# A fused linear-attention and gated-MLP kernel on one core: in blocks 3 to 6, four of the seven products of a Strassen-type step are summed in one PSUM half bank

## The chip, the cores and the metric

The kernel runs on one NeuronCore of one Trainium2 chip. The metric is the device time of one execution in microseconds, as the median of several runs. Of the kernel before there are three runs: 1049.51, 1049.64 and 1049.84 us, median 1049.64 us. One more execution was taken with the hardware profiler; it took 1050.2 us, of which 1048.4 us lie between its first and its last instruction (the span).

## The reference

Random-feature attention, then a gated MLP without an activation. All data are float32.

```
attention: q, k, v are (8 batches, 8 heads, 576 tokens, 64), omega is (128, 64)
  phi(x) = exp(h - max(h)) / sqrt(128),  h = x omega^T - |x|^2 / 2,  x = q or k, scaled by 64^-0.25
  kv = phi(k)^T v      z = sum over tokens of phi(k)
  out = phi(q) kv / (phi(q) z + 1e-6)
MLP: x is the attention's output as (4608 tokens, 512)
  y = ((x w_a) * (x w_b)) w_out,   w_a and w_b are 512 x 1536, w_out is 1536 x 512
```

## The kernel before

**Blocks.** The MLP runs over blocks of 512 tokens on TensorE (PE), one for each of the eight batches (b = 0 to 7), and a ninth (b = 8) that gathers the last 64 tokens of every batch. Every float32 operand is split into a high and a low part, and a product is made of three matmuls (high x high, high x low, low x high). Blocks 0 and 1 (`moe_block`, L1188) multiply plainly. Blocks 2 to 8 (`moe_block7`, L1263) form the two inner products x w_a and x w_b, in 2 x 2 sub-blocks of 256, by a Strassen-type scheme with seven products in place of eight. The sums of the weights that the scheme needs are made once (`weight_sums`, L1230), stored in DRAM and loaded again by every unit (tiles `t` and `bq`); the sums of the tokens are the tiles `Sa` and `Sb`.

**A unit** (`unit`, L1273) is one pair of 128-wide feature groups of one of the two weights: 12 units in a block. Each of its seven products (`product`, L1293) is six matmuls of 128 x 256 into one half (256 columns) of one of two PSUM banks, `p0` and `p1` (`halves`). The products of all units form one chain in their order (list `prev`), and each also waits until everything that reads its bank so far has read it (`pb.readers`, L1302). The order in a unit is: first into p0 half 0, copied by ScalarE (ACT) to the SBUF tile `c4` (L1313); second into p1 half 0 and third into p1 half 1; a VectorE (DVE) add of 512 columns over p1 (L1317); fourth into p0 half 1 and fifth into p0 half 0; a DVE add of 512 and one of 256 columns over p0 (L1326, L1328); sixth and seventh into p1, and a DVE add of 512 columns (L1333). So a unit has one ACT copy and four DVE adds, and the four results stand in `c4`.

**Items.** After both units of a pair, DVE multiplies the two `c4` (L1358), the result is split into `ghl` (L1361, `hilo` L1181), and eight items are put into a list `left`: an item is three matmuls of 128 x 512 that multiply `ghl` by `wo` into the output banks `o` (`Out.mm`, L1010). `flush` (L1220) takes items out of the list in order and gives them to the planner at certain places of a unit: L1320 (1, or 5 in the first unit of a block), L1329 (1) and L1335 (2; in blocks 7 and 8 it is 1), none in the last unit of a block. Blocks 7 and 8 use another output (`Out7`, L1049), whose items are products of six matmuls of 128 x 256, and one product `one` (L1126, in list `ones7`) that goes into `p1` in the midst of the next unit and needs the tile `wo`.

**Attention.** The attention for the next batches is done in bursts (`burst`, L685) that are put between units at places fixed in the table `PLACE`. A burst holds the numerator of an earlier pair (L878), kv (L804), and the projections of 8 chunks of 128 tokens (`four`, L528, twice, 16 matmuls each). Bursts 12 to 31 (`MERGED`) use `p0` and `p1` for the first `four` and stand in the chain of products; ACT (or DVE) copies the projections out of them. At the last head pair of a batch (hp1 == 0, L717) the burst also makes the projections of the next batch's last tokens, `last_chunks` (L675), a third call of `four` on banks of its own (`ppke` and `ppqe`, ring `at`), which the planner places where it finds room; the next burst waits for it (`carry["e"]`, L688).

**The order of the work** is made by a planner on the host (`Graph`, L63 to L296) when the kernel is built. Every operation has a cost in ns (`mm` L299 for matmuls, `dve` and `act` for the others), engines that may run it, a priority and its dependences. The planner simulates the engines with these costs, always starts what can start first and breaks ties by priority (PE) or by due time (DVE, ACT, POOL), plans four times and keeps the plan whose simulated end is earliest. The program issues each engine's instructions in that order; on the chip an engine's queue is in order. Between a projection burst and other work the planner prefers the next piece of the same burst, up to 700 ns (`GLUE`).

The lines that the text speaks of most:

```
def mm(n, cols):
    return n * max(112, 7 + 0.441 * cols)
...
flush(seq + 3, 5 if i == w == 0 else k)
...
if hp1 == 0:
    last_chunks(b1, pr + 15, xe, sqe, lead, mg)
```

## Time and profile before

| what | value |
|---|---|
| median of three runs | 1049.64 us (1049.51 to 1049.84) |
| the profiled execution | 1050.2 us |
| its span, first to last instruction | 1048.4 us |
| PE busy (matmuls) | 1034.0 us, 99% of the span |
| DVE busy | 899.6 us, 86% |
| ACT busy | 588.9 us, 56% |
| mean granted clock of PE | 0.994 |
| DMA | 314.16 MB, 300 GB/s |

The profiled execution stands 0.6 us above the median of the runs. A matmul's end is modelled in the profile: the difference between two starts tells how fast PE goes, the duration of one does not. Busy shares are means over stages, so the profile is read by block: blocks 2 to 8 begin at about 300, 411, 523, 634, 746, 849 and 947 us.

### The profile page before, as it was taken

How to read it: one execution, taken by the hardware profiler on the slowest of the kernel's cores; microseconds unless marked ns; L12 is line 12 of the kernel's file. 1: busy time of each engine (PE TensorE's matmuls, PEld its weight loads, DVE VectorE, ACT ScalarE, POOL GpSimd, SP SyncE). 2: the span in 40 equal slices, each digit the busy share in tenths (PEclk: the TensorE clock that was granted, in tenths of full speed). 3: DMA queues.
4: the chain of work that ended last, by engine and by line, in shares of the span. 5: the costliest groups of instructions: out<-in, count | busy, mean ns of one | idle time of the engine just before them, and what ended most of it. 6: DMA issues, size and time to landing. Idle time of an engine off the chain costs nothing.

```text
span 1048.4 us, 22053 instructions
## 1 busy us (share of the span) xinstructions
PE 1034.0 (99%) x7806; PEld 916.1 (87%) x7806; DVE 899.6 (86%) x2255; ACT 588.9 (56%) x1629; POOL 109.5 (10%) x177
## 2 busy tenths in 40 slices
PE   9999999999999999999999999999999998999998
PEld 8877777777788988999999998899989998999998
DVE  6999999899997889888998888888887666999876
ACT  8989798868565646765566556654552023233221
POOL 0112111202101111111111111101010000000000
PEclk9989999999999999999999999999999999999999
DMA  9857878898989999998899988998788787899981
GB/s 353 324 200 249 294 237 261 313 330 297 306 304 384 355 286 323 325 352 301 302 311 357 311 303 268 352 304 291 254 310 280 262 277 256 309 359 349 367 323 49
DMA packets 123647, 314.16 MB, mean 300 GB/s; under 512 B 17680, under 2 KB 40976, under 8 KB 123536
## 3 DMA queue, kind: packets, MB, share of 16 engines
q1 hardware_dynamic: 122656, 312.10, 85.7%
q8 instruction: 61, 1.00, 0.4%
q10 hardware_dynamic: 880, 0.66, 0.2%
q14 instruction: 50, 0.41, 0.1%
HBM read 255.52 MB, written 57.18 MB: 298 GB/s over the span
## 4 chain that ended last, share of the span: by engine, by line
PE 82%; DVE 12%; DMA 2%; issue 2%; ACT 2%; DVEq 0%; ACTq 0%
PE p L1298 39%; PE o L1016 18%; PE o_P L1086 5%; PE pa L1206 3%; PE pb L1206 3%; PE ppk L540 3%; PE pkv L804 2%; PE pm L878 2%; PE p L540 2%; DVE sm L565 1%; DMA td<-ts 1%; DVE raw L419 1%; DVE zero L824 1%; PE p L1086 1%; PE pn L950 1%
## 5 line engine op out<-in xcount | busy, mean ns | idle before, releaser
L1308 DVE TENSOR_TENSOR c<-p,c 128x512 f32<-128x512 f32 (+1 forms) x336 | 207.6, 618 | 69.6 <-PE p L1298 56.2
L1016 PE MATMUL o<-wo,ghl 128*128 128x512 f32 x1008 | 249.5, 393 | 0.0
L1016 PEld LDWEIGHTS o<-wo,ghl 128*128 128x128 f32 x1008 | 183.5, 188 | 37.7 <-issue 0.9
L1298 PE MATMUL p<-Sa,t 128*128 128x256 f32 x1008 | 132.6, 280 | 0.7 <-ACT c L365 0.7
L1298 PEld LDWEIGHTS p<-Sa,t 128*128 128x128 f32 x1008 | 124.5, 188 | 1.3 <-ACT c L365 1.1
L758 POOL TENSOR_TENSOR z<-hk 128x256 f32<-128x256 f32 x56 | 46.1, 824 | 632.7 <-ACT hk L578 496.9
L834 ACT ACTIVATE hq<-hq,dn 128x128 f32<-128x128 f32 x224 | 70.1, 390 | 45.1 <-DVE dn L830 44.9
L365 ACT COPY c<-p 128x256 f32<-128x256 f32 x84 | 31.1, 370 | 102.1 <-PE p L1298 98.9
L1206 PE MATMUL pa<-x,wa 128*128 128x512 f32 x288 | 76.2, 408 | 2.1 <-DVE x L373 2.1
L1206 PE MATMUL pb<-x,wb 128*128 128x512 f32 x288 | 74.9, 403 | 0.6 <-ACT wb L365 0.3
L1298 PE MATMUL p<-x,t 128*128 128x256 f32 x504 | 74.3, 283 | 0.9 <-ACT oc L365 0.7
L1298 PE MATMUL p<-Sb,bq 128*128 128x256 f32 x504 | 74.3, 283 | 0.0
L1298 PE MATMUL p<-Sb,t 128*128 128x256 f32 x504 | 73.5, 282 | 0.0
L578 ACT ACTIVATE hq<-hq,sm 128x128 f32<-128x128 f32 x192 | 64.4, 392 | 15.3 <-DVE sm L573 15.2
L824 DVE CUSTOM_DVE_ANT_0 zero<-hq,zb 128x128 bf16<-128x128 f32 x224 | 69.2, 309 | 1.0
L1298 PE MATMUL p<-x,wa 128*128 128x256 f32 x504 | 69.1, 283 | 0.2 <-DVE c L1308 0.2
L1298 PE MATMUL p<-x,wb 128*128 128x256 f32 x504 | 69.0, 282 | 0.0
L1298 PEld LDWEIGHTS p<-x,wa 128*128 128x128 f32 x504 | 65.3, 188 | 3.7 <-DVE c L1308 0.8
L1206 PEld LDWEIGHTS pa<-x,wa 128*128 128x128 f32 x288 | 54.4, 193 | 16.0 <-DVE x L373 2.4
L1298 PEld LDWEIGHTS p<-x,t 128*128 128x128 f32 x504 | 66.5, 190 | 2.0 <-ACT oc L365 0.9
L1298 PEld LDWEIGHTS p<-x,wb 128*128 128x128 f32 x504 | 65.2, 189 | 3.1 <-DVE c L1308 0.4
L1206 PEld LDWEIGHTS pb<-x,wb 128*128 128x128 f32 x288 | 53.2, 189 | 15.4 <-DVE a L1214 1.1
(202 smaller groups left out, 2025.5 us busy)
## 6 DMA issues: line engine op xcount, KB each, us to landing
t<-td SPq DMA_DIRECT2D x168, 512.0 KB
wo<-wod SPq DMA_DIRECT2D x96, 512.0 KB
bq<-bd SPq DMA_DIRECT2D x84, 256.0 KB
qdr<-qd SPq DMA_DIRECT2D x112, 160.0 KB
hq<-qdr SPq DMA_DIRECT2D x28, 640.0 KB
X<-in_kqt_dram SPq DMA_DIRECT2D x30, 512.0 KB
raw<-in_wab_dram SPq DMA_DIRECT2D x24, 512.0 KB
td<-ts SPq DMA_DIRECT2D x24, 512.0 KB
```

The lines of the kernel that those rows point to most:

```text
L365: nc.scalar.copy(o(), i())
L540: nc.tensor.matmul(flat4(pps[w])[:, c * M:c * M + M], x()[rows, c * P:c * P + P], om.ap[rows], start=True, stop=True)
L578: g.op({"ACT": 392}, lambda e, c=c, w=w, to=to, at=at: nc.scalar.activation(to.ap[:, at + c], src[w](c), AF.Exp, scale=SC, bias=sm.ap[:, 2 ...
L758: g.op({"POOL": pool2(n)}, lambda e: nc.gpsimd.tensor_tensor(o(), a(), c(), op=ALU.add), r=r, w=w, alloc=list(al), prio=pri, deps=zload[-1 ...
L804: nc.tensor.matmul(pkv.ap[D * j:D * j + D, 0:M], vb.ap[:, vc, 0:D], c(), start=(n == 0), stop=(n == 4))
L824: g.op({"DVE": 413}, lambda e, c=c, j=j, rr=rr, qc=qc: nc.vector.tensor_tensor_reduce(out=junk.ap[rr], in0=qc(), in1=zb.ap[rr, j], scale=1 ...
L834: g.op({"ACT": 392}, lambda e, c=c, src=src: nc.scalar.activation(hq.ap[:, c], src(), AF.Copy, scale=dn.ap[:, c:c + 1]), r=[sd, (dn, None) ...
L1016: nc.tensor.matmul(po.ap[:], ghl.ap[:, gi, t * P:(t + 1) * P], wo.ap[:, wi], start=(n == 0 and i == 0), stop=(n == NF - 1 and i == 2))
L1086: nc.tensor.matmul(pb.ap[:, t], A[0](ai)[:, t * P:(t + 1) * P], W[0](wi), start=begin and t == j == 0, stop=stop and t == 1 and j == 2)
L1206: nc.tensor.matmul(pb.ap[:], wt.ap[:, wi, c], xs[c].at(xi), start=(c == 0 and i == 0), stop=(c == NC4 - 1 and i == 2))
L1298: nc.tensor.matmul(pb.ap[:, half], wcol(wi, c), xc(xi, c), start=n == 0, stop=n == 5)
L1308: g.op({"DVE": dve(n)}, lambda e: nc.vector.tensor_tensor(c4.ap[:, o], pb.ap[:, half], y(), op=ALU.add), r=[*((pb, k) for k in range(half. ...
```

## The change

Three things are changed. The new settings `PSH`, `PSUMS`, `PLO`, `SUBX` and `SNAP` stand at 0 or empty, and what hangs on them is as before.

1. In blocks 3 to 6 (`CHAIN`) a unit's products go another way. First, sixth, seventh and eighth step below all go into p0 half 0 without clearing it, so that the bank holds a running sum; after each, ACT copies the half bank to one quarter of `c4` (four copies of 256 columns). The other three go into p1, and DVE adds them to `c4` (one add of 512 columns, one of 256). The first unit of such a block gives the planner 3 items at L1320 where it gave 5; the others give what they gave.
2. `last_chunks` gets the banks `p0` and `p1` in merged bursts and stands in the chain right behind the burst's second `four`. This holds for bursts 15, 19, 23 and 27.
3. The planner's cost of a matmul: 117.8 ns for 256 columns (119.9 before) and 228.3 ns for 512 (232.8 before), for all blocks.

```diff
 def mm(n, cols):
-    return n * max(112, 7 + 0.441 * cols)
+    return n * (117.8 if cols == 256 else max(112, 4 + 0.438 * cols))
...
-            def product(pb, half, wcol, wr, xc, xrd, pos):
+            def product(pb, half, wcol, wr, xc, xrd, pos, begin=True):
...
-                            nc.tensor.matmul(pb.ap[:, half], wcol(wi, c), xc(xi, c), start=n == 0, stop=n == 5)
+                            nc.tensor.matmul(pb.ap[:, half], wcol(wi, c), xc(xi, c), start=begin and n == 0, stop=n == 5, skip_group_check=not begin)
...
+            if b not in CFG["CHAIN"]:
...
+            def snap(q, al=()):
+                g.op({"ACT": act(HM), **{k: dve(HM) for k in CFG["SNAP"]}}, copier(lambda: c4.ap[:, q], lambda: p0.ap[:, 0]), r=[(p0, 0)], w=[(c4, q)],
+                     alloc=list(al), prio=-12)
+            def add(o, half, parts):
+                n = HM * (half.stop - half.start)
+                g.op({"DVE": dve(n)}, lambda e: nc.vector.tensor_tensor(c4.ap[:, o], p1.ap[:, half], c4.ap[:, o], op=ALU.add),
...
+            wait = 3 if i == w == 0 else 0
+            def first():
+                steps.append(product(p0, 0, lambda k, c: f0.ap[:, k, c], (f0, None), xcol(0, lo_half), xr(0), 0))
+                snap(0, [c4])
+            def second():
+                product(p1, 0, lambda k, c: f0.ap[:, k, 2 + c], (f0, None), xcol(2, lo_half), xr(2), 1)
+            def sixth():
+                product(p0, 0, tcol(tA, 0), (tA, None), scol(1), sr[0], 2, False)
+                snap(2)
+            def fifth():
+                product(p1, 1, tcol(tA, 1), (tA, None), scol(0), sr[0], 4)
+            def seventh():
+                product(p0, 0, tcol(tB, 0), (tB, None), scol(2), sr[1], 5, False)
+                snap(3)
+            first()
...
+                second()
+                sixth()
+                flush(seq + 3, wait or k)
+                fifth()
+                seventh()
+            add(slice(0, 4, 3), slice(0, 2), (0, 3))
             flush(seq + 6, k)
+            product(p0, 0, tcol(tB, 1), (tB, None), xcol(2, hi_half), xr(2), 7, False)
+            snap(1)
+            product(p1, 1, lambda k, c: bq.ap[:, k, P * c:P * c + P], (bq, None), scol(3), sr[1], 8, False)
+            add(slice(2, 3), slice(1, 2), (2,))
...
             if hp1 == 0:
-                last_chunks(b1, pr + 15, xe, sqe, lead, mg)
+                last_chunks(b1, pr + 15, xe, sqe, [*lead, *chain()], mg, banks() if merged else None)
+                glue(place if merged else None, carry["e"])
+                if merged:
+                    carry.pop("e")
```

## Rows read from the trace of the kernel before

**Rows 1.** The page's head: the span, and the busy time, share and instructions of each engine.

```profile
span 1048.4 us, 22053 instructions
PE 1034.0 (99%) x7806; PEld 916.1 (87%) x7806; DVE 899.6 (86%) x2255; ACT 588.9 (56%) x1629; POOL 109.5 (10%) x177
```

**Rows 2.** Busy time of each engine by stage (from:to, length, then busy us and number of instructions), the granted clock of PE (1.00 is 2.4 GHz, 0.50 is 1.2 GHz), the DMA share and GB/s. Blocks 2, 3, 4, 5, 6 and 7.

```profile
300.20:410.80 110.60, 109.66 (x893) 98.47 (x891) 94.13 (x246) 68.05 (x195) 13.95 (x24) 1.00 0.95 326
410.80:522.70 111.90, 111.90 (x906) 101.11 (x906) 96.47 (x265) 67.75 (x193) 13.77 (x24) 1.00 0.92 324
522.70:634.10 111.40, 111.40 (x906) 101.13 (x905) 96.82 (x262) 65.17 (x189) 14.33 (x24) 1.00 0.92 317
634.10:745.70 111.60, 111.60 (x906) 101.00 (x905) 95.47 (x258) 61.99 (x183) 15.13 (x24) 1.00 0.90 303
745.70:848.90 103.20, 103.20 (x769) 93.57 (x768) 74.30 (x169) 34.68 (x99) 4.39 (x6) 1.00 0.83 279
848.90:946.60 97.70, 94.44 (x739) 91.70 (x739) 82.84 (x171) 29.31 (x66) 0.00 (x0) 0.98 0.87 303
```

**Rows 3.** Whom PE waited for in the whole execution: us in total, times, longest. The largest rows that bear on the change.

```profile
PE p L1086 <- DMA wo<-wod: 2.1, 1, 2.1
PE pa L1206 <- DVE x L373: 2.1, 1, 2.1
...
PE p L1298 <- ACT c L365: 0.7, 1, 0.7
PE p L1298 <- ACT oc L365: 0.7, 1, 0.7
```

**Rows 4.** PE's matmuls in blocks 3 to 6 (410.8 to 848.9 us), grouped: busy us and mean ns of one, then PE's idle time just before them.

```profile
L1016 PE MATMUL o<-wo,ghl 128*128 128x512 f32 x577 | 143.2, 394 | 0.0
L1298 PE MATMUL p<-Sa,t 128*128 128x256 f32 x576 | 75.5, 280 | 0.0
```

**Rows 5.** DVE and ACT in blocks 3 to 6, in the same form: the DVE adds of a unit, its ACT copy, and three frequent neighbours on ACT.

```profile
L1308 DVE TENSOR_TENSOR c<-p,c 128x512 f32<-128x512 f32 x145 | 99.1, 683 | 33.9 <-PE p L1298 30.0 <-ACT hq L834 1.1 <-ACT hq L578 1.0
L1308 DVE TENSOR_TENSOR c<-p,c 128x256 f32<-128x256 f32 x48 | 19.8, 413 | 0.8
...
L365 ACT COPY c<-p 128x256 f32<-128x256 f32 x48 | 17.6, 368 | 48.5 <-PE p L1298 45.5 <-DVE c L1358 2.7
L834 ACT ACTIVATE hq<-hq,dn 128x128 f32<-128x128 f32 x120 | 37.6, 390 | 30.1 <-DVE dn L830 30.1
L365 ACT CAST ghl<-c 128x512 fp32r<-128x512 f32 x16 | 9.9, 620 | 14.7 <-PE o L1016 10.1 <-issue 3.0 <-DVE c L1358 1.4
```

**Rows 6.** One unit on PE in block 4, in order of time: start us, length us, what. The first row is two products, the second two, the next two one each; the fifth is four items, and the last begins the next unit.

```profile
563.59 1.58 PE L1298 MATMUL p<-x,wa 128*128 128x256 f32 x12
565.01 1.57 PE L1298 MATMUL p<-Sa,t 128*128 128x256 f32 x12
566.41 0.88 PE L1298 MATMUL p<-Sb,t 128*128 128x256 f32 x6
...
567.84 0.88 PE L1298 MATMUL p<-Sb,bq 128*128 128x256 f32 x6
568.56 2.88 PE L1016 MATMUL o<-wo,ghl 128*128 128x512 f32 x12
571.28 1.56 PE L1298 MATMUL p<-x,wb 128*128 128x256 f32 x12
```

**Rows 7.** From a product to its ACT copy, and from an ACT copy to the product that waited for it: timelines of PE and of ACT in block 2. The bracket is the engine's idle time before, and what ended it.

```profile
321.05 1.60 PE L1298 MATMUL p<-x,wa 128*128 128x256 f32 x12
...
321.96 0.37 ACT L365 COPY c<-p 128x256 f32<-128x256 f32 x1 [0.92 <-PE p L1298]
...
316.31 0.35 ACT L365 COPY c<-p 128x256 f32<-128x256 f32 x1
...
316.71 0.97 PE L1298 MATMUL p<-Sa,t 128*128 128x256 f32 x6 [0.69 <-ACT c L365]
```

**Rows 8.** The end of burst 19's pair, nine items, the last tokens' projections (`ppke`, `ppqe`) and three items, on PE; and ACT's copies of the burst's first `four` out of p0 and p1 (`hk<-p`, `hq<-p`).

```profile
559.20 0.27 PE L540 MATMUL ppq<-om,X 64*128 64x128 f32 x1
559.40 2.36 PE L1016 MATMUL o<-wo,ghl 128*128 128x512 f32 x9
561.69 0.37 PE L540 MATMUL ppke<-om,Xe 64*128 64x128 f32 x1
...
562.46 0.27 PE L540 MATMUL ppke<-om,Xe 64*128 64x128 f32 x1
...
562.57 0.27 PE L540 MATMUL ppke<-om,Xe 64*128 64x128 f32 x1
...
562.78 0.97 PE L1016 MATMUL o<-wo,ghl 128*128 128x512 f32 x3
...
558.65 0.59 ACT L365 COPY hk<-p 128x512 f32<-128x512 f32 x1 [0.74 <-issue]
559.13 0.59 ACT L365 COPY hq<-p 128x512 f32<-128x512 f32 x1
```

**Rows 9.** Stages as in rows 2, around the two longest waits of PE: right after the wait at 53.8 us, and right after the one that ends at 873.75 us.

```profile
54.00:58.00 4.00, 4.00 (x10) 3.12 (x11) 3.97 (x10) 3.74 (x11) 0.81 (x2) 0.50 0.46 161
...
873.75:876.00 2.25, 1.57 (x9) 1.37 (x10) 0.00 (x0) 0.58 (x1) 0.00 (x0) 0.80 0.90 331
876.00:878.10 2.10, 2.10 (x11) 2.10 (x11) 0.00 (x0) 0.00 (x0) 0.00 (x0) 0.50 0.34 124
```

More of the change, by code (lines that the diff above doesn't have):

```diff
@@ L528, in four @@
     def four(nm, b, pri, x, xdep, dst, c0, sm, sq, al, deps, mg, more, banks=None):
-        own = banks is None
+        own, less = banks is None, b in CFG["SUBX"]
         pps = [g.buf("at", [P, 4 * M], F32, f"pp{'kq'[w]}{nm}{c0}", more) for w in range(2)] if own else banks
@@ L574, in four @@
         g.op({"DVE": 300}, biases, r=[(sm, (c0, 0)), (sm, (c0, 1)), (psq if sq is None else sq, None)], w=[(sm, (c0, 0)), (sm, (c0, 1))], prio=pri + 2)
-        for w in range(2):
+        for w in range(2) if less else ():
+            to, at = dst[w]
+            whole = (lambda pp=pps[w]: wide4(pp)) if not (b >= B1 or not own) else (lambda to=to, at=at: to.ap[:, at + c0:at + c0 + 4])
+            mine = lambda to=to, at=at: to.ap[:, at + c0:at + c0 + 4]
+            done = [(to, at + c) for c in some]
+            g.op({"DVE": dve(4 * M)}, lambda e, w=w, whole=whole, mine=mine: nc.vector.tensor_tensor(
+                mine(), whole(), sm.ap[:, 2, w, sl].unsqueeze(2).to_broadcast([P, 4, M]), op=ALU.subtract),
+                r=[*held[w], (sm, (c0, w))], w=done, prio=pri + 3 + w)
+            g.op({"ACT": act(4 * M)}, lambda e, mine=mine: nc.scalar.activation(mine(), mine(), AF.Exp, scale=SC), r=done, w=done, prio=pri + 3 + w)
+        for w in range(0 if less else 2):
             for c in some:
@@ L1231, in weight_sums @@
         pr = 500000
+        pool = lambda n: {"POOL": pool2(n)} if CFG["PSUMS"] else {}
         hb = [wab_b[2 * i + k, w] for k in range(2)]
@@ L1303, in product @@
                 return prev[-1]
-            def add(o, pb, half, y, rd, wr):
-                n = HM * (half.stop - half.start)
-                g.op({"DVE": dve(n)}, lambda e: nc.vector.tensor_tensor(c4.ap[:, o], pb.ap[:, half], y(), op=ALU.add),
-                     r=[*((pb, k) for k in range(half.start, half.stop)), *((c4, k) for k in rd)], w=[(c4, k) for k in wr], prio=-12)
-            both, twice = slice(0, 2), lambda k: c4.ap[:, k:k + 1].to_broadcast([P, 2, HM])
-            steps.append(product(p0, 0, lambda k, c: f0.ap[:, k, c], (f0, None), xcol(0, lo_half), xr(0), 0))
@@ L1322, in unit, with add_old @@
[L1322 to L1328 removed]
+            if b not in CFG["CHAIN"]:
+                def add_old(o, pb, half, y, rd, wr):
+                    n = HM * (half.stop - half.start)
+                    g.op({"DVE": dve(n)}, lambda e: nc.vector.tensor_tensor(c4.ap[:, o], pb.ap[:, half], y(), op=ALU.add),
+                         r=[*((pb, k) for k in range(half.start, half.stop)), *((c4, k) for k in rd)], w=[(c4, k) for k in wr], prio=-12)
+                both, twice = slice(0, 2), lambda k: c4.ap[:, k:k + 1].to_broadcast([P, 2, HM])
+                steps.append(product(p0, 0, lambda k, c: f0.ap[:, k, c], (f0, None), xcol(0, lo_half), xr(0), 0))
+                g.op({"ACT": act(HM)}, copier(lambda: c4.ap[:, 3], lambda: p0.ap[:, 0]), r=[(p0, 0)], w=[(c4, 3)], alloc=[c4], prio=-10)
+                product(p1, 0, lambda k, c: f0.ap[:, k, 2 + c], (f0, None), xcol(2, lo_half), xr(2), 1)
+                product(p1, 1, tcol(tA, 0), (tA, None), scol(1), sr[0], 2)
+                add_old(slice(0, 4, 2), p1, both, lambda: twice(3), [3], [0, 2])
+                k = 0 if i == NFP - 1 and w else 1
+                flush(seq + 3, 5 if i == w == 0 else k)
+                product(p0, 1, tcol(tA, 1), (tA, None), scol(0), sr[0], 4)
+                if ones7 and w == 0:
+                    ones7.pop(0)(MOE + seq + 5)
+                product(p0, 0, tcol(tB, 0), (tB, None), scol(2), sr[1], 5)
+                add_old(slice(1, 3), p0, both, lambda: twice(2), [2], [1, 2])
+                add_old(slice(3, 4), p0, slice(1, 2), lambda: c4.ap[:, 1:2], [1], [3])
+                flush(seq + 6, k)
+                product(p1, 0, tcol(tB, 1), (tB, None), xcol(2, hi_half), xr(2), 7)
+                product(p1, 1, lambda k, c: bq.ap[:, k, P * c:P * c + P], (bq, None), scol(3), sr[1], 8)
+                add_old(slice(1, 3), p1, both, lambda: c4.ap[:, 1:3], [1, 2], [1, 2])
+                flush(seq + 9, (k and not (b == B and i == NFP - 1)) if seven else 2 * k)
+                return
@@ new lines, in fifth @@
+            def fifth():
[4 more added lines that the diff above has]
+            first()
+            if ones7 and w == 0:
+                ones7.pop(0)(MOE + seq + 0.5)
+                sixth()
[3 more added lines that the diff above has]
+                fifth()
+            else:
+                second()
+                sixth()
+                flush(seq + 3, wait or k)
+                fifth()
+                seventh()
```

40 lines of the change are left out of this document (18 added, 22 removed).

## The prediction

> **What bounds the kernel now.** I read the page's head first: PE is busy for 99% of the span, DVE for 86%, ACT for 56% [rows 1]. Since a matmul's end is modelled, I asked next, stage by stage, whether PE has any idle time where the change lies. In blocks 3 to 6, from 410.8 to 848.9 us, PE is busy for the whole of each stage and its granted clock is 1.00, that is 2.4 GHz [rows 2]; its groups of matmuls there have 0.0 us of idle time before them [rows 4]. Busy could still hide a slow pace, so I looked at the starts in one unit: twelve products' matmuls take 565.01 - 563.59 = 1.42 us, the next twelve 1.40 us, six take 0.72 us, and twelve matmuls of 512 columns take 571.28 - 568.56 = 2.72 us [rows 6]. That is 118 ns for 256 columns and 227 ns for 512, with nothing lost between products and none between products and items. So in the four blocks that the chain touches, PE alone sets the time, and DVE, though busy for 72 to 87% of them [rows 2], holds nobody up. What the kernel loses on PE, it loses elsewhere: 2.1 us at the start of block 0, 0.7 us in block 2, and 2.1 + 0.7 us where block 7 takes over from block 6 [rows 3].
>
> **The chain itself.** The number of matmuls and their columns stay: seven products of six in each unit, before and after. PE's floor in blocks 3 to 6 stays too.
>
> *DVE.* A unit now has three adds of 512 columns and one of 256: 3 x 683 + 413 = 2.46 us [rows 5]. After, it has one of each: 1.10 us. That takes 1.37 us from each of 48 units, 66 us in all. I cost the gain at nothing, because PE waits for no DVE add in these blocks [rows 4]; DVE merely gets idle. If that cover is wrong, PE would have shown idle time, and it shows none.
>
> *ACT.* Three more copies of 368 ns [rows 5] in 48 units add 53 us. In block 3 ACT goes from 67.8 to 67.8 + 12 x 3 x 0.368 = 81 us of 111.9, in block 6 from 34.7 to 48 of 103.2 [rows 2]. It doesn't become the bound. What counts is that the copies now stand between products: the next product into p0 must wait for the copy of the one before.
>
> *The wait that is added.* A product's six matmuls take 0.71 us [rows 6]. An ACT copy that was waiting started 321.96 - 321.05 = 0.91 us after its product's first matmul [rows 7], 0.20 us after the last column went in. It takes 0.37 us, and PE went on 316.71 - (316.31 + 0.35) = 0.05 us after such a copy [rows 7]. So PE needs 0.62 us from the end of a product into p0 to the next one there. Three of the four copies in a unit have one product in p1 between, 0.71 us: covered, with 0.09 us to spare. The fourth, after the seventh product, has none; it needs one item, 2.72 / 4 = 0.68 us [rows 6]. The last product also waits for DVE's add over p1: 0.20 + 0.37 + 0.05 + 0.68 + 0.05 = 1.35 us after the seventh product, against 0.68 + 0.71 = 1.39 us of an item and the eighth product. All of this fits by less than 0.1 us, if ACT and DVE are free at that moment. Four items fall to a unit, of which one is needed in the hole and up to three can fill where a copy comes late. Behind a waiting copy ACT's own queue stands still: projections' exponentials and quotients (390 ns each) and splits of `ghl` (620 ns) [rows 5]; the `ghl` splits are what the items need, so a held queue can in the end starve PE of its filler.
>
> The planner knows these waits when it orders the work, and PE takes whatever can start first. So below I bound the cost by 0 (every hole filled) and by 48 x 0.62 = 30 us for the uncovered copy alone with no item ever ready. I take 0, because the nearest row, the same units with four DVE adds on an engine with less idle time, shows 0.0 us of waits over 438 us [rows 4].
>
> *Items held back.* The first unit of each chained block puts in 3 items in place of 5, so 2 x 4 = 8 more are still unplaced when block 7 starts. PE does the same items later; they are a reserve for the holes. I cost it at nothing within blocks 3 to 6. At the turn to block 7 it can go either way (rivals).
>
> **The last tokens' projections.** They stand alone now. Nine items before them take 561.69 - 559.40 = 2.29 us where 9 x 0.227 = 2.04 would do, and the projections take 562.78 - 561.69 = 1.09 us, though eight pairs at 0.11 us (562.46 to 562.57) are 0.88 us; the three items behind take 563.59 - 562.78 = 0.81 in place of 0.68 us [rows 6, 8]. Of the 0.25 us of the nine items, one such 0.13 belongs to leaving the pair and stays. Beside the pair they cost 0.88 us, so a place saves 0.12 + 0.21 + 0.13 = 0.46 us; four places (bursts 15, 19, 23, 27) save 1.8 us. Against that: they need p0 and p1, which the first `four` has just filled. ACT's two copies end at 559.13 + 0.59 = 559.72 us, while the pair's last matmul starts at 559.20 and the projections could follow at 559.31 [rows 8]: with ACT doing both copies, PE waits 0.05 + 0.41 = 0.46 us, and nothing is saved; DVE, which may take one of them, would free the banks in time. Bounds 0 and -1.8 us; I take the middle, -0.9 us. Afterwards the next product needs those two banks copied out again, some 0.20 + 0.59 + 0.48 us; the nine items that now stand between pair and projections cover it. Without them, four times 1.3 us would be lost.
>
> **The planner's costs.** 117.8 and 228.3 ns are nearer to what rows 6 shows than 119.9 and 232.8. No instruction is added, but every engine's order is planned anew, in blocks 0 to 2, 7 and 8 too. No row prices that. It can move the waits of rows 3: none below 0, and their kind can come again elsewhere. I take 0.
>
> **Sum.** 1050.2 us of the profiled execution - 0.9 = 1049.3; that execution stands 0.6 us above the median of the runs, so the forecast is **1048.7 us**. About 0.2%, 2.1 us, is what a measurement of this kernel can tell from no change.
>
> **Rivals.**
>
> *1. Faster: the turn to block 7 is mended.* PE waits 2.1 us for a `wo` load there and 0.7 us for an ACT copy behind it [rows 3], and then goes slowly: granted clock 0.80 for 2.25 us and 0.50 (1.2 GHz) for 2.10 us [rows 9], which costs 0.20 x 2.25 + 0.50 x 2.10 = 1.5 us. Together 4.3 us. For it: a new plan with eight items in reserve, and true costs of a matmul by which a load is issued in time. Against: the load waits for the items of block 6 that hold its buffer, and these now come later. If all of it goes: 1048.7 - 4.3 = 1044.4 us; half of it is 1046.5. The wait at 53.8 us, with half clock behind it [rows 3, 9], is of the same kind and could move too, but almost nothing of the change reaches that far forward.
>
> *2. Slower: ACT comes late.* A copy that finds ACT in an operation of 390 or 620 ns [rows 5] is late by some 0.25 us, half of one, less 0.09 us of room. Where no item is ready, PE waits. Per copy that is a little; of 192 copies, one in ten late by 0.25 us without filler gives 19 x 0.25 = 4.8 us: 1053.5 us. From about 12 such copies on it would decide (3 us eat the gain and the 2.1 us). For: no reserve of more than 0.1 us, ACT busy for up to 73% of a block. Against: today's plan holds its moments to within nothing that shows on PE [rows 4].
>
> *3. Slower through the clock.* The row first: the two times the clock fell to 0.50, PE had just idled for 2.1 us [rows 3, 9]; the 0.7 us wait for an ACT copy in block 2 left that block at 1.00 [rows 2, 3]. If short waits in every unit did it, one stretch such as that at 876 us costs 1.0 us, and four of them bring 1053 us. The Trainium skill ("TensorE: Matmul & The Clock Gate", section "A second HAM failure mode: psum-queue depth-cycling") says that a kernel that cycles through PSUM banks and idles for a moment between groups of matmuls lets the clock swing between its two levels, and loses throughput by it. By that rule this change, which ties every unit to one bank, would be slower; no run here shows it yet.
>
> *4. It doesn't do what it says:* the last tokens' projections may wait for ACT at every one of their four places and save nothing; then it is 1049.6 us, within the same band.
>
> **Chances.** My forecast, with rival 4, 0.43: its own range is 1047.5 to 1051.7 us. Rival 1: 0.34. Rival 2: 0.20, rival 3: 0.03. These are the chances of no change by over 0.2%, of faster and of slower (0.23). The range takes in rival 1 whole and rival 2 at its price: 1044.0 to 1053.5 us. Outside lie many unfilled holes, or both long waits gone.
>
> **What would show it.** Right: in blocks 3 to 6 PE's products have no idle time with <-ACT c; 192 ACT copies of 368 ns and 96 DVE adds over p1; between the seventh and the eighth product stand three or more matmuls of an item; DVE's busy time falls by about 66 us and ACT's rises by about 53. `ppke` follows the pair's last `ppq` within 0.15 us. Wrong: waits of PE for ACT c in dozens (rival 2), a clock below 1.00 in a chained block (rival 3), or a block of a length other than today's. If the time moves by over 2 us while blocks 3 to 6 keep their 438.1 us, the new plan outside them did it: look at the waits at 53.8 and 873.75 us.

## The result and the profile after

The changed kernel takes **1059.1 us** (median of 4 runs, 1056.6 to 1061.5) against 1049.6 us of the kernel before in the same session: a ratio of 1.009, with a 95% interval of 1.007 to 1.0109. It is slower by 0.9%; I had forecast 1048.7 us, and the result lies above my range. The profiled execution took 1059.66 us with a span of 1057.9 us, 9.5 us over the span of before. The four executions took 1061.5, 1059.7, 1058.5 and 1056.6 us at mean granted clocks of 0.994, 0.996, 0.998 and 1.000, so what one profile shows must be read beside the median.

The head of the page after, as [rows 1]:

```profile
span 1057.9 us, 22150 instructions
PE 1037.8 (98%) x7806; PEld 913.8 (86%) x7806; DVE 843.6 (80%) x2143; ACT 646.3 (61%) x1789; POOL 111.4 (11%) x177
```

The change does what it says to the engines: DVE loses 56 us, ACT gains 57, PE has the same 7806 matmuls. Now the stages, as in [rows 2] (from:to, length, busy us and number on PE, PEld, DVE, ACT and POOL, granted clock, DMA share, GB/s): up to block 2, blocks 2 to 6, block 7, block 8, and blocks 3 to 6 by themselves. "PEld" is PE's weight loads.

```profile
0.00:303.20 303.20, 294.10 (x1881) 231.12 (x1882) 284.42 (x737) 246.40 (x662) 49.55 (x75) 0.99 0.83 289
...
303.20:849.60 546.40, 546.22 (x4349) 489.76 (x4348) 395.65 (x1077) 347.81 (x1007) 61.84 (x102) 1.00 0.90 308
849.60:955.60 106.00, 99.99 (x757) 95.69 (x756) 84.76 (x174) 29.35 (x66) 0.00 (x0) 0.98 0.84 288
955.60:1052.80 97.20, 97.20 (x823) 97.08 (x822) 77.72 (x156) 22.69 (x56) 0.00 (x0) 1.00 0.77 276
...
414.20:849.60 435.40, 435.31 (x3451) 390.30 (x3451) 302.61 (x836) 279.61 (x814) 47.45 (x78) 1.00 0.88 303
```

The same stages before:

```profile
0.00:300.20 300.20, 294.65 (x1881) 232.41 (x1882) 281.84 (x738) 239.72 (x650) 47.90 (x75) 0.99 0.83 290
...
300.20:848.90 548.70, 547.76 (x4373) 495.29 (x4372) 457.18 (x1194) 297.65 (x859) 61.58 (x102) 1.00 0.90 310
848.90:946.60 97.70, 94.44 (x739) 91.70 (x739) 82.84 (x171) 29.31 (x66) 0.00 (x0) 0.98 0.87 303
946.60:1043.40 96.80, 96.80 (x817) 96.54 (x816) 76.63 (x153) 22.25 (x55) 0.00 (x0) 1.00 0.74 273
```

The lengths differ by +3.0, -2.3, +8.3 and +0.4 us. But blocks 2 to 6 now hold 4349 matmuls in place of 4373: 24 item matmuls have gone on into block 7 (its items went from 36 matmuls to 60). At 0.227 us each [rows 6] that is 5.4 us moved. Like for like:

- **start, blocks 0 and 1: +3.0 us.** PE does the same 1881 matmuls and idles 303.20 - 294.10 = 9.1 us in place of 5.55.
- **blocks 2 to 6, where the chain is: +3.1 us.**
- **block 7, which the diff does not touch: +2.9 us.** PE idles 6.0 us in place of 3.3.

PE's waits after, as in [rows 3]:

```profile
PE p L1317 <- DVE c L1328: 3.8, 4, 1.9
PE pb L1224 <- ACT a L365: 2.6, 1, 2.6
PE p L1104 <- DMA wo<-wod: 1.4, 1, 1.4
PE pa L1224 <- DVE wa L373: 1.2, 1, 1.2
```

The first row lies in block 7, the second and fourth in the start. Asked for blocks 3 to 6 alone, the same view has no row, and the groups of matmuls there read as in [rows 4], with no idle time:

```profile
L1317 PE MATMUL p<-x,t 128*128 128x256 f32 x288 | 42.7, 284 | 0.0
```

So where do the 3.1 us of the chain show? In the starts. The unit on PE in block 4 (as [rows 6]; `p<-Sb,t` is the seventh product, `p<-x,t` the eighth, three matmuls `o<-wo` are an item):

```profile
582.05 1.66 PE L1317 MATMUL p<-x,wa 128*128 128x256 f32 x12
583.55 1.58 PE L1317 MATMUL p<-Sa,t 128*128 128x256 f32 x12
584.96 0.91 PE L1317 MATMUL p<-Sb,t 128*128 128x256 f32 x6
585.71 0.86 PE L1034 MATMUL o<-wo,ghl 128*128 128x512 f32 x3
586.41 0.90 PE L1317 MATMUL p<-x,t 128*128 128x256 f32 x6
587.14 0.86 PE L1034 MATMUL o<-wo,ghl 128*128 128x512 f32 x3
```

The first two products take 583.55 - 582.05 = 1.50 us in place of 1.42, the seventh 0.75, the eighth 0.73 in place of 0.71. Nothing stands still for long, yet many turns into a bank lose some hundredths. Summed over the trace from each matmul's start to that of the next, the products of blocks 3 to 6 take 244.1 us, before 240.5: +3.6. Of these 0.9 us each lie at the second and the eighth product, 0.8 at the first, 0.6 at the seventh. (The first product's share is in part something else: nine first products come right behind a burst's projections and lose 0.10 us each, before five.) Why that is, the weight loads and ACT tell for the eighth product (two views of the same stretch, the bracket is the idle time before):

```profile
586.33 0.77 PEld L1317 LDWEIGHTS p<-x,t 128*128 128x128 f32 x6 [0.20 <-ACT c L365]
```

```profile
585.91 0.37 ACT L365 COPY c<-p 128x256 f32<-128x256 f32 x1 [0.54 <-PE p L1317]
```

The seventh product's last column goes in at 584.96 + 0.75 = 585.71; ACT starts to copy 0.20 us later, is done at 586.28, the weights of the eighth are loaded from 586.33 on, and its first matmul starts at 586.41. The waits are there after all, on the weight loads. In blocks 3 to 6 after (us in total, times, longest):

```profile
PEld pkv L898 <- issue: 8.0, 28, 0.3
PEld p L1317 <- ACT c L365: 6.5, 32, 0.2
```

and before, where no product's load waits for ACT's `c`:

```profile
PEld pkv L880 <- issue: 8.0, 28, 0.3
...
PEld p L1298 <- DVE c L1308: 0.3, 1, 0.3
```

Nearly all of the 6.5 us after lie at the eighth product, where an item stands between (busy us and mean ns of one, then idle time and what ended it):

```profile
L1317 PEld LDWEIGHTS p<-x,t 128*128 128x128 f32 x288 | 38.3, 188 | 7.7 <-ACT c L365 6.2
```

The 0.08 us that the first two products lose are no turn into p0. They belong to the second product, which goes to p1 and waits until DVE has added the last product of the unit before:

```profile
582.25 0.42 DVE L1366 TENSOR_TENSOR c<-p,c 128x256 f32<-128x256 f32 x1
```

The add ends at 582.67 and the second product's first weights are loaded from 582.73 on. The same stands at ten of the 48 second products, each with its load 0.05 us after the add's end, and it makes up their 0.9 us.

**Block 7.** Beside PE's wait for `wo` that was there before, DVE waits for `wo` in block 7 after (us in total, times, longest); before it has no such row:

```profile
DVE owr L1050 <- DMA wo<-wod: 4.4, 2, 2.3
```

DVE's queue (`owr<-wo` is a sum over a `wo` tile for the output weights), then PE beside it:

```profile
914.36 1.42 DVE L373 TENSOR_TENSOR og<-ogf,og 128x256 fp32r<-128x256 f32 x4
918.12 0.69 DVE L1050 TENSOR_TENSOR owr<-wo 128x512 f32<-128x512 f32 x1 [2.34 <-DMA wo<-wod]
918.73 0.68 DVE L1328 TENSOR_TENSOR c<-p,c 128x512 f32<-128x512 f32 x1
```

```profile
916.69 0.87 PE L1317 MATMUL p<-Sb,t 128*128 128x256 f32 x6
919.47 1.11 PE L1317 MATMUL p<-x,t 128*128 128x256 f32 x6 [1.90 <-DVE c L1328]
920.38 1.49 PE L1317 MATMUL p<-Sb,bq 128*128 128x256 f32 x6
```

DVE stands for 2.34 us before a sum whose `wo` tile has not landed. The add that frees the product's bank is the next in the queue, and PE waits 1.90 us for it. The same comes again at 952.05 (DVE waits 2.05 us, PE 1.58). No row of block 7 before is of this kind.

**The last tokens' projections** are not beside the pair. In block 4 nine item matmuls still stand between, that is three items (where [rows 8] and the prediction say nine and three items, they are nine and three matmuls):

```profile
562.76 0.27 PE L542 MATMUL ppq<-om,X 64*128 64x128 f32 x1
562.96 2.33 PE L1034 MATMUL o<-wo,ghl 128*128 128x512 f32 x9
565.23 1.16 PE L542 MATMUL p<-om,Xe 64*128 64x128 f32 x16
566.32 0.97 PE L1034 MATMUL o<-wo,ghl 128*128 128x512 f32 x3
```

566.32 - 565.23 = 1.09 us, as before [rows 8]. The planner keeps its margin of 1200 ns on what these projections wait for, and that now includes ACT's copies out of p0 and p1; so it puts them some 2.3 us later, where they always were.

### The profile page after: what moved, and what is told of

It reads as the page before. It is cut to its first block, busy times and chain, and to the rows that moved or that the text cites. A ratio compares the mean times of both kernels' runs of the same rounds, so it can differ in the third digit from the quotient of the medians.

```text
span 1057.9 us, 22150 instructions
## 1 busy us (share of the span) xinstructions
PE 1037.8 (98%) x7806; PEld 913.8 (86%) x7806; DVE 843.6 (80%) x2143; ACT 646.3 (61%) x1789; POOL 111.4 (11%) x177
## 4 chain that ended last, share of the span: by engine, by line
PE 83%; DVE 5%; DMA 3%; ACT 1%; issue 1%; DVEq 0%; ACTq 0%
PE p L1317 37%; PE o L1034 21%; PE pb L1224 5%; PE pa L1224 5%; PE o_P L1104 4%; PE pm L896 3%; PE pkv L822 2%; PE ppk L542 2%; PE p L542 2%; DMA wo<-wod 2%; DMA otd<-ot 1%; PE p L1104 1%; DVE c L1328 1%; DMA natee<-in_kqnt_dram 1%; DVE zero L842 0%
## 5 line engine op out<-in xcount | busy, mean ns | idle before, releaser
L1034 PE MATMUL o<-wo,ghl 128*128 128x512 f32 x1008 | 268.7, 396 | 0.4 <-DVE ghl L373 0.4
L1034 PEld LDWEIGHTS o<-wo,ghl 128*128 128x128 f32 x1008 | 176.4, 188 | 31.8 <-DVE ghl L373 1.6
L365 ACT COPY c<-p 128x256 f32<-128x256 f32 x228 | 84.5, 371 | 188.3 <-PE p L1317 155.5
L1328 DVE TENSOR_TENSOR c<-p,c 128x512 f32<-128x512 f32 (+1 forms) x144 | 89.0, 618 | 28.7 <-PE p L1317 27.0
L1366 DVE TENSOR_TENSOR c<-p,c 128x512 f32<-128x512 f32 x96 | 52.9, 551 | 54.5 <-ACT c L365 38.5
L842 DVE CUSTOM_DVE_ANT_0 zero<-hq,zb 128x128 bf16<-128x128 f32 x224 | 71.8, 321 | 2.1
L1317 PEld LDWEIGHTS p<-Sb,bq 128*128 128x128 f32 x504 | 68.4, 190 | 2.8
L1317 PEld LDWEIGHTS p<-Sb,t 128*128 128x128 f32 x504 | 67.1, 188 | 2.4 <-ACT c L365 0.2
```

The costliest lines, as they stand in the source:

```text
L365: nc.scalar.copy(o(), i())
L842: g.op({"DVE": 413}, lambda e, c=c, j=j, rr=rr, qc=qc: nc.vector.tensor_tensor_reduce(out=junk.ap[rr], in0=qc(), in1=zb.ap[rr, j], scale=1 ...
L1034: nc.tensor.matmul(po.ap[:], ghl.ap[:, gi, t * P:(t + 1) * P], wo.ap[:, wi], start=(n == 0 and i == 0), stop=(n == NF - 1 and i == 2))
L1317: nc.tensor.matmul(pb.ap[:, half], wcol(wi, c), xc(xi, c), start=begin and n == 0, stop=n == 5, skip_group_check=not begin)
L1328: g.op({"DVE": dve(n)}, lambda e: nc.vector.tensor_tensor(c4.ap[:, o], pb.ap[:, half], y(), op=ALU.add), r=[*((pb, k) for k in range(half. ...
L1366: g.op({"DVE": dve(n)}, lambda e: nc.vector.tensor_tensor(c4.ap[:, o], p1.ap[:, half], c4.ap[:, o], op=ALU.add), r=[*((p1, k) for k in ran ...
```

## The experiments

Theory **C**: the chain costs 3 to 4 us by its turns in p0. Rival theories on the other 6 us: **H**, the items held back starve block 7; **P**, the new costs are bad for the planner; **L**, any new plan is a new draw, and this one happens to be worse at the start and in block 7. The columns: median time, ratio to the kernel before with its 95% interval, start of block 2, and the products' time (start to start, in the profiled run) in blocks 3 to 6 and in block 7.

| kernel | us | ratio | block 2 at | products 3 to 6 | block 7 |
|---|---|---|---|---|---|
| before | 1049.6 | 1 | 300.2 | 240.5 | 62.2 |
| after | 1059.1 | 1.0090 [1.0070, 1.0109] | 303.2 | 244.1 | 66.1 |
| e1 after, 5 items | 1061.9 | 1.0112 [1.0092, 1.0131] | 306.8 | 245.7 | 64.5 |
| e2 after, old costs | 1055.3 | 1.0047 [1.0031, 1.0064] | 298.1 | 244.7 | 61.9 |
| e4 after, no chain | 1056.3 | 1.0053 [1.0037, 1.0070] | 300.7 | 240.7 | 64.2 |
| e3 before, new costs | 1054.0 | 1.0037 [1.0023, 1.0050] | 304.5 | 240.0 | 65.2 |
| e5 before, 256 cost only | 1046.5 | 0.9958 [0.9940, 0.9977] | 299.9 | 240.3 | 62.8 |
| e6 before, 512 cost only | 1051.3 | 0.9999 [0.9985, 1.0013] | 299.3 | 241.4 | 62.3 |
| e7 before, 0.4409 for 0.441 | 1053.3 | 1.0025 [1.0010, 1.0041] | 300.8 | 241.2 | 61.2 |
| e8 e2 with 60 ns margin | 1052.8 | 1.0027 [1.0010, 1.0044] | 303.1 | 242.1 | 62.4 |
| e9 after, start held | 1052.2 | 1.0026 [1.0010, 1.0042] | 302.2 | 243.7 | 62.6 |
| e10 before, new costs, start held | 1053.1 | 1.0028 [1.0012, 1.0045] | 300.5 | 240.8 | 65.3 |
| e11 e9, `wo` sums later | 1055.2 | 1.0052 [1.0034, 1.0069] | 301.7 | 244.6 | 63.7 |
| e12 before, projections beside | 1052.2 | 1.0019 [1.0004, 1.0034] | 300.8 | 240.2 | 63.9 |
| e13 after, 117.9 ns | 1059.4 | 1.0095 [1.0075, 1.0115] | 305.2 | 245.3 | 63.4 |
| e14 after, 117.78 ns | 1053.7 | 1.0042 [1.0027, 1.0058] | 299.0 | 243.7 | 62.7 |
| e15 after, old costs, start held | 1054.7 | 1.0051 [1.0034, 1.0068] | 301.3 | 245.0 | 61.5 |
| e16 after, `wo` sums later | 1057.3 | 1.0073 [1.0054, 1.0091] | 304.2 | 244.0 | 62.4 |

"Start held" means that the planner had to use the old kernel's order on every engine for the work of blocks 0 to 2. Those runs put block 2 at 300.5 to 302.2 us with the same order of work, so a single profile's start is sure to about 2 us.

**e1_flush5: nothing held back.** Edit:

```
-            wait = 3 if i == w == 0 else 0
+            wait = 5 if i == w == 0 else 0
```

> The changed kernel, but the first unit of a chained block again gives 5 items to the planner (as before the change) in place of 3, so none is held back. Theory H (items held back make the wo loads of block 7 late; DVE then stands at a sum of weights that waits for wo, with the adds of the products queued behind it, and PE waits for them 1.9 and 1.6 us): both waits PE <- DVE c of over 1 us in block 7 go, block 7's products take 62 us again in place of 66.1, and the time falls by 3 to 4 us, to about 1055.5. Rival C (the chained ACT copies themselves cost the time): no change, 1059 us within 1. Rival S (the new plan of the start costs it): no change behind 303 us either, though the start may come out by 1 to 3 us another way, since everything is planned anew.

Block 7 had its 36 item matmuls again, and PE still waited 3.4 us there for DVE's `c` (longest 2.3). H falls: the items held back lengthen block 7, but do not make its waits. In blocks 3 to 6 PE's matmuls now wait 1.5 us for ACT's `c` (three times), where after has no such wait: there the held items may be worth something, which one plan can't settle.

**e2_oldcost: the old costs in the changed kernel.**

```
-    return n * (117.8 if cols == 256 else max(112, 4 + 0.438 * cols))
+    return n * max(112, 7 + 0.441 * cols)
```

> The changed kernel, but with the planner's matmul costs of before (119.9 and 232.8 ns); the chain, the held-back items and the moved projections stay. Rival S (new costs give another order in blocks 0 and 1, with PE waits of 2.6 + 1.2 + 1.1 + 1.0 + 0.9 us that were not there): block 2 begins at 300 us in place of 303, and the time falls by 3 us to about 1056. Theory H and rival C: it stays at 1059 within 1.5 us, and block 7's waits for DVE stay.

Start and block 7 lost their harm, and the chain's blocks kept theirs (244.7 us): two causes, as C says, and the second comes with the plan.

**e3_cost_alone: the new costs in the old kernel** (the edit of e2 the other way).

> The kernel before with the planner's new matmul costs alone. Rival S: block 2 begins 3 us later, 1052.5 us. Theory H and rival C: 1049.6 us within 1.5, since neither the chain nor the held-back items are in it.

4 us slower with no other change, by block 2 at 304.5 and block 7's waits for DVE's `c` (2.6 us); its products in blocks 3 to 6 are as before. My "planner's costs: I take 0" was wrong.

**e4_no_chain: after, with `CHAIN=()`.**

> The changed kernel without the chain (blocks 3 to 6 as before, 5 items in the first unit), with the new costs and the moved projections. Rival C: blocks 3 to 6 lose the 3.6 us that their products now take more (244.1 us against 240.5), and nothing else; 1055.5 us. Theory H: those 3.6 us, and the 3.9 us of block 7 as well, about 1052; what is left over 1049.6 is the start's. The moved projections alone are worth 0 to -1.8 us.

Products of blocks 3 to 6 fall from 244.1 to 240.7 us, and the time by 2.8 us. The chain is that term. What is left, 1.0053, has the new costs and the moved projections, and in block 7 DVE waits for `wo` again (3.1 us) and PE for DVE's `c` (2.5 us).

**e5_cost256, e6_cost512, e7_jitter: the old kernel with one cost changed.** e5 takes only 117.8 ns for 256 columns, e6 only `4 + 0.438 * cols` for 512, e7:

```
-    return n * max(112, 7 + 0.441 * cols)
+    return n * max(112, 7 + 0.4409 * cols)
```

> The kernel before, but the planner's cost of a 256-column matmul is 117.8 ns (new) and that of a 512-column one 232.8 (old). Theory P (a wrong cost misleads the planner: the 228.3 ns for 512 columns, below the 237 to 261 ns that a pa or pb matmul takes in blocks 0 and 1, is what spoils the start): blocks 0 and 1 end at 300 us as before, and the time is 1050 within 1.5. Rival L (lottery: any change of a cost gives another plan whose losses fall elsewhere): it can come out anywhere from 1048 to 1056, with waits of PE in blocks 0 and 1 at other places than before.

> The kernel before, but the planner's cost of a 512-column matmul is 228.3 ns (new) and that of a 256-column one 119.9 (old). Theory P: the start loses its 3 to 4 us again (block 2 at 303 to 304.5 us) and the time is 1053 to 1054. Rival L: anywhere from 1048 to 1056, and not tied to which of the two costs is new.

> The kernel before with a cost of 232.74 in place of 232.79 ns for 512 columns and 119.87 in place of 119.90 for 256: 0.02%, far below what any row could tell from the truth. Theory P: 1050 within 1, since the cost is as right or wrong as before. Rival L: the plan changes anyway, and the time differs from the kernel before by more than 2 us, most likely upwards, with waits of PE of over 1 us at new places in blocks 0, 1 or 7.

Each half of the costs is harmless or better alone (0.9958 and 0.9999), both together are 1.0037, and a change of 0.02%, which can carry no knowledge, is 1.0025. PE's order differs in e7 from its 178th matmul on, at 19.7 us. Where e7's 2.6 us go is not shown: its profile is of the fastest of its eleven executions (1050.1 us, granted clock 1.000), and its stages are as good as those of before. P falls as I had put it, one wrong cost that spoils the start, and L is there; whether the two new costs together make a worse plan likelier is taken up below, under e13 and e14. e5 is faster than both kernels, by 0.42% of before; its eight executions have mean granted clocks of 0.996 to 1.000, where the 30 of before in its session have 0.991 to 0.997. That goes with the gain, and no term of its profile that I found explains more than the draw, so I don't call it a gain of the cost.

**e8_chain_margin: e2, and the planner told that a chained product's operand comes 60 ns later than it thinks.**

```
-                                 prio=MOE + seq + pos, deps=...
+                                 prio=MOE + seq + pos, margin=60 if b in CFG["CHAIN"] else 0, deps=...
```

> The kernel of e2_oldcost (chain, held-back items and moved projections with the old costs), but the planner reckons 60 ns more for every wait of a chained product on ACT or DVE, so that it puts an item or another product where it now lets the copy arrive in the last tens of ns. Theory C (the chain's cost in blocks 3 to 6, products 244.7 us there against 240.5, is many waits of 10 to 40 ns where the room is under 0.1 us): the first matmul of products 2, 3, 5 and 6 takes 118 to 122 ns where it took 130 to 150, and the products of blocks 3 to 6 fall to 241.5 us or less. Rival X (it is the switching between products and items, or a slower pace of a chained product): they stay at 244 or rise, as more items stand between products.

The products of blocks 3 to 6 fell from 244.7 to 242.1 us, and the loads' waits for ACT from 37 (8.3 us) to 3:

```profile
PEld p L1317 <- ACT c L365: 1.3, 3, 0.8
```

The loss is a turn that was planned too tight, and not too little work to fill it: with an item put in where the margin asks for one, most of it goes. It is 0.6 us short of what I expected. Of the four first matmuls named, those of the second and the sixth product in order (the eighth by name) fell to 121 and 120 ns on average, from 127 and 156 in e2; those of the third and the fifth stayed at 129 and 132.

**e9_pin_after, e10_pin_cost: after, and the old kernel with the new costs, both with the start held.** The edit lists the old order and lets the planner choose freely from block 3 on:

```
+                    if o.n < PIN_N and PIN[e][went[e]] != o.n:
+                        continue
```

In e9 the projections that lie in block 2, in the held part, stay in banks of their own.

> The changed kernel, but the planner is held to the old kernel's order for blocks 0 to 2 (the new costs, the chain and the moved projections stay in blocks 3 to 8). If the 3.0 us at the start came from a new draw of the plan there, block 2 starts at about 300.2 us again in place of 303.2, and the time is about 1059.1 - 3 = 1056 us, with products in blocks 3 to 6 at about 244 us (240.5 before). If the chain reached back into blocks 0 to 2 in some other way, block 2 starts at 300 and the time stays at 1059, the loss showing up later. Block 7's products: 62 us if its waits were a matter of the draw, 65 to 66 if they come with the costs or the chain.

> The old kernel with the two new costs of a matmul, held to the old order in blocks 0 to 2: no chain, projections where they were. If what the costs alone lost (1054.0 us against 1050.2) was the draw of the plan in blocks 0 to 2, the time is 1049 to 1050.5 us with block 2 at 300.2. If block 7 loses its 3 us again (products there 65 us, waits for DVE c), 1052 to 1053. The run with chain and new costs under the same start minus this one is the price of the chain and the moved projections alone: 3 to 5 us if the chain's waits cost what blocks 3 to 6 showed, 0 if the whole loss is the plan's draw.

e9 is 1.0026: with the old start, the whole change costs 2.7 us in place of 9.5, less than I had expected, for block 7 came out well too (62.6). Blocks 3 to 6 still have 243.7 us of products. e10 keeps the good start and loses 2.8 us to waits for DVE's `c` in block 7, so it is no faster than e9: the difference of the two, which I had meant as the chain's price, mixes the chain with a draw in block 7 and says nothing.

**e11_pin_owr: e9, with the `wo` sums later.**

```
-  r=[(wo[k], None)], w=[(wr, k)], ..., prio=-7, deps=gate)
+  r=[(wo[k], None)], w=[(wr, k)], ..., prio=-7, deps=gate, margin=3000)
```

> As the changed kernel with blocks 0 to 2 held, and the planner told that DVE's sum of a wo tile may only be queued 3 us after the load is planned to land. If block 7's waits of 1.9 and 1.6 us come from DVE's queue standing behind that sum while a load is late, PE's waits for DVE c go there, products of block 7 take about 62 us in place of 66, and the time is about 3 us below the run with blocks 0 to 2 held alone. If the late load itself holds PE (its items miss it), the wait moves to PE <- DMA wo and nothing is gained.

A miss: e9 has no long wait for DVE's `c` in block 7, so there was nothing to take away. The kernel came out slower than e9, with 1.3 us of such waits in block 7. The test had to be made where the wait is (e16).

**e12_pin_beside0: the projections really beside the pair.** Old kernel, start held, p0 and p1 lent to the projections at three places, and their margin 0:

```
-                last_chunks(b1, pr + 15, xe, sqe, lead, mg)
+                last_chunks(b1, pr + 15, xe, sqe, [*lead, *chain()], 0, banks())
```

> The old kernel (old costs, no chain), blocks 0 to 2 held to the old order, with the last tokens' projections of bursts 19, 23 and 27 really put right behind the pair's, in p0 and p1, with no margin of the plan on what they wait for. If a place saves the 0.46 us that I worked out, three save 1.4 us of PE's time in blocks 4 to 6 and the time is about 1048.8 us. If PE waits there for ACT's two copies, as my bound of 0 says, the three places show a wait of about 0.4 us for ACT or DVE each, and blocks 4 to 6 keep their length (111.4, 111.6, 103.2 us) and the time 1050.2.

```profile
561.28 0.27 PE L600 MATMUL ppk<-om,X 64*128 64x128 f32 x1
561.29 0.27 PE L600 MATMUL ppq<-om,X 64*128 64x128 f32 x1
561.40 1.63 PE L600 MATMUL p<-om,Xe 64*128 64x128 f32 x16
562.96 3.03 PE L1080 MATMUL o<-wo,ghl 128*128 128x512 f32 x12
```

They follow the pair at once and then take 562.96 - 561.40 = 1.56 us in place of 1.09: PE stands in the middle of them, its weight loads waiting for ACT (`hq`, 0.2 us at each of the three places). The 0.46 us are given back where I had put the bound of 0. The three places lie in blocks 3 to 5 (at 450.27, 561.40 and 673.21 us), not in 4 to 6 as the expectation has it; these blocks take 111.8, 111.8 and 111.7 us against 111.9, 111.4 and 111.6.

**e13_redraw, e14_redraw2: the changed kernel with another draw.** `117.8` was made 117.9 in e13 and 117.78 in e14.

> The changed kernel with the planner's 117.8 ns for 256 columns made 117.9: 0.08% of one cost, the same work and instructions, another order of PE from its 43rd row on. If the loss outside blocks 3 to 6 is the draw of the plan, this lands elsewhere than 1059.1: within 1051 to 1060 us, with block 2 starting anywhere from 298 to 305 us and block 7's products anywhere from 62 to 66 us. If the loss there is caused by the change itself, it comes again: block 2 at 303 us, block 7's products at 66 us, 1059 us. Products of blocks 3 to 6 keep 244 us in both cases.

> A second such draw: 117.8 made 117.78. Same expectations: by the draw 1051 to 1060 us with start and block 7 anywhere, by the change itself 1059 us with block 2 at 303 and block 7's products at 66. Products of blocks 3 to 6 at 244 us in both.

One lands at 1059.4, the other at 1053.7 us: 5.8 us between two kernels that differ by 0.1% in one of the planner's numbers. The chain's blocks show their 244 to 245 us in both. That is L, with C beside it.

It does not clear the new costs. DVE's wait for `wo` in block 7 (3 to 4.4 us, and 2.3 to 3.8 us of PE's waits for DVE's `c` with it) comes in six of the eight kernels that plan with both of them and have no edit to that sum: after, e1, e3, e4, e10 and e13, but not e9 and e14. Of the eight with an old cost only e12 has it (2.0 us; 0.2 or less in the others). So a plan is a draw, and the new costs may well make this loss a likelier one.

**e15_pin_chain: the chain and the projections, old costs, start held.**

> The chain and the moved projections with the old costs of a matmul, and blocks 0 to 2 held to the old order: the change without its costs and without a new draw at the start. If the chain costs what its added waits cost in blocks 3 to 6 (3.2 to 3.6 us of products), the time is 3 to 4 us over the old kernel with block 2 at 300 to 302 us; with 10 items fewer in blocks 3 to 6 and as many more in block 7. If the new costs matter within blocks 3 to 6, the products there differ from the 243.7 us of the run with new costs by over 1 us.

1.0051 (3.6 to 7.1 us slower). The products of blocks 3 to 6 take 245.0 us, with 41 waits of the loads:

```profile
PEld p L1378 <- ACT c L425: 9.6, 41, 0.6
```

That is 4.5 us over before, without any new costs and with the old start. Blocks 3 to 6 hold 8 items fewer than before, not 10.

**e16_owr: after, with the edit of e11.**

> The changed kernel, the order of PE the same up to the last third of block 7's approach, with one more condition for the planner: DVE's sums of a wo tile may only be queued 3 us after the load is planned to land. If PE's two waits for DVE c in block 7 (1.9 and 1.6 us) come from DVE's queue standing behind such a sum while the load is late, they go: products of block 7 at 62 to 63 us in place of 66.1, time 3 us below 1059.1. If the late load holds PE in any case, the waits come again under another name and the time stays.

PE's order is that of after up to 853.5 us, 2.9 us into block 7. From there the sum comes when its tile has landed, and DVE does not stand:

```profile
918.22 0.75 DVE L373 TENSOR_TENSOR og<-ogf,og 128x256 fp32r<-128x256 f32 x2
918.89 0.68 DVE L1050 TENSOR_TENSOR owr<-wo 128x512 f32<-128x512 f32 x1
919.50 0.69 DVE L1328 TENSOR_TENSOR c<-p,c 128x512 f32<-128x512 f32 x1
```

```profile
PE p L1317 <- DVE c L1328: 1.5, 4, 0.8
```

Block 7's products take 62.4 us in place of 66.1 and the block 102.3 in place of 106.0: in the profile 3.7 us, as expected. Half of it is PE's idle time (6.0 us, now 4.1); the other half is pace, for the granted clock of the block is 1.00 in place of 0.98. The time, 1.0073 against 1.009, moved by less, and the two intervals overlap; that DVE's queue was block 7's wait rests on the trace.

## Why the prediction was wrong

**The step that failed first is "The planner's costs ... No row prices that ... I take 0".** I had said that a new plan could move the waits of [rows 3], and then gave that no price and no case of its own on the slow side; rival 1 took the same freedom as a gain. In fact a change of 0.02% in the costs moves the time by 2.6 us (e7), and one of 0.1% by 5.8 us (e13 against e14). With the old order held up to block 2, the changed kernel is at 1.0026 in place of 1.009 (e9): of the 9.5 us some 6 come with the new plan outside the chain. By the profile they are the 3.0 us of the start, sure to about 2 us, and the 2.9 us of block 7, which e9 was free to plan anew. "Almost nothing of the change reaches that far forward" was wrong as well: PE's order differs from that of before from its 267th matmul on, at 29.8 us.

**The second is a term of the chain: 0.62 us from the end of a product to the next one in p0, of which I took 0.05 us between copy and product.** That 0.05 came from one row [rows 7], and one in which PE had stood idle for 0.69 us: there the weight load starts with its matmul, at 316.71.

```profile
316.71 0.77 PEld L1298 LDWEIGHTS p<-Sa,t 128*128 128x128 f32 x6 [1.12 <-ACT c L365]
```

In the trace after, in 75 of the 192 turns (those where the next product into p0 starts within 0.26 us of the copy's end), ACT starts its copy 0.20 us after the last column (median; ACT was free, as I had said), takes 0.37, and the matmul starts 0.13 us after the copy's end, 0.05 of it before the weight load: **0.70 us**. Against a product's 0.71 us, and an item's 0.68, that leaves 0.01 us behind a product and nothing behind an item, where I had counted 0.09 us of room. The load, which else runs about 0.11 us ahead of its matmul (581.94 for the matmul at 582.05), starts only when the bank is free. The Trainium skill ("TensorE: Matmul & The Clock Gate", section "Architectural detail: the array is 16× 32×32, not 1× 128×128") says that PE can pull weight loads ahead of matmuls in flight; the rows agree, and they show that the load of a matmul that has to wait for its bank is held back with it (586.33, after the copy's end at 586.28). The prediction also has no term for the turn in p1, from the last product over DVE's add of 256 columns to the next unit's second product: 0.9 us. What the chain costs in all: 3.6 us of products in after; 243.7 to 245.7 us in every kernel with the chain and no margin, 240.0 to 241.4 in every one without. My bounds (0 to 30 us) held it, but I chose 0 by a row, [rows 4], that cannot show it: idle time of PE's matmuls is 0.0 there after as well.

- *DVE and ACT.* As forecast: 192 copies of 370 ns, 48 adds of 512 and 48 of 256 columns, and neither engine the bound. In blocks 3 to 6 DVE loses 60 us (66 forecast), ACT gains 50 (53).
- *Rival 2* had the right place, but not the cause: 8 of the 192 copies start over 0.25 us later than the 0.20 us, where its price took 19. The loss is of some hundredths in many turns.
- *Rival 3, the clock.* False: 1.00 in blocks 3 to 6, all 435.4 us. The rule of the Trainium skill ("TensorE: Matmul & The Clock Gate", section "A second HAM failure mode: psum-queue depth-cycling") that I weighed there is not met in this trace; it speaks of idle moments between groups of matmuls, and the matmuls of these blocks show none.
- *Rival 1.* The wait for `wo` at the turn fell from 2.1 to 1.4 us and the wait for ACT's copy behind it stayed at 0.7; new waits of 3.8 us behind them ate that.
- *The projections.* -0.9 us was wrong. Rival 4's nothing came, though by the planner's margin: in after they do not stand beside the pair at all, and where they do (e12) PE waits for ACT in the middle, as rival 4 says.
- *Items held back.* They make no wait in block 7 (e1). That they are worth nothing within blocks 3 to 6, as costed, is not shown (e1).

What stays open: the chain's price in whole time. By products it is 3.2 to 4.5 us in the held runs (e9, e15), by time 2.7 and 5.3 us, with intervals that overlap. The kernels that contain the chain, without margin and with no start held or sum moved (after, e1, e2, e13, e14), lie at 1.0042 to 1.0112; those without it (before, e3 to e7) at 0.9958 to 1.0053. Their means are some 7 us apart, more than the products' 3.6 us, so some of the loss outside blocks 3 to 6 may come with the chain as well. Why the new plan's start is worse was not traced to one decision. That small changes of the costs move it is shown by the redraws (305.2 us in e13, 299.0 in e14); how much of it is chance and how much the new costs, so few plans can't tell.

## What to carry to other kernels

Where a planner orders the work, any edit of its costs is a new draw of every stage: measure that spread first (a cost changed by 0.02%, or the old order held outside the edited part), and give it a term and a range in the forecast. A turn-around that is planned to within 0.1 us needs its price from many rows, with the weight load in it; look at the weight loads' waits, for the matmuls' own idle time can read 0.0 while each turn loses a few hundredths. And when an engine waits for an add, look at the head of that engine's queue: the add was ready, and the sum ahead of it was waiting for a load.

## What the runs showed of the hardware

A short wait need not show as a wait of matmuls: in blocks 3 to 6 the products lost 3.6 us of pace, their matmuls show no idle time there, and what shows are 32 waits of 0.2 us on weight loads. And the clock fell after one of two like waits in block 7: after the 1.90 us before 919.47 a stretch ran at 0.50 (1.2 GHz), after the 1.58 us before 953.40 none did:

```profile
920.40:921.60 1.20, 1.20 (x7) 1.20 (x7) 1.20 (x3) 0.00 (x0) 0.00 (x0) 0.50 1.07 428
...
953.40:956.00 2.60, 2.60 (x22) 2.60 (x23) 2.60 (x6) 1.14 (x2) 0.00 (x0) 1.00 1.03 418
```
